# Four interleaved attention layers on one core: 288 score columns per unit in both sliding layers, cut as large bursts in 32x64 tiles and one small burst

## The chip, the cores and the metric

The kernel runs on one core of one Trainium2 chip. The metric is device time in microseconds (us) of one execution; lower is better. The core has a matrix engine (TensorE, PE in the profile, with its weight loads listed apart as PEld), a vector engine (DVE), a scalar engine (ACT), GpSimd (POOL) and a queue engine (SP) that issues DMAs. Each engine plays a list of instructions in a fixed order and waits on semaphores for the others.

## The reference

x is 2048 tokens by 512 features in bfloat16. Four residual layers follow one another: linear attention A, sliding-window attention B, A again with the same weights, B again. Each normalises x first. There are 32 heads of 16 features, and the window of B is 256 tokens.

```python
def _B_ref(x, wqkv, wo):
    B, S, D = x.shape
    H = 32; Dh = D // H; W = 256
    qkv = (lambda x, *d: x.transpose(*d))((x @ wqkv).reshape(B, S, 3, H, Dh), 2, 0, 3, 1, 4)
    q, k, v = qkv[0], qkv[1], qkv[2]
    scores = jnp.einsum("bhqd,bhkd->bhqk", q, k) * (Dh ** -0.5)
    idx = jnp.arange(S)
    mask = (idx[:, None] - idx[None, :] >= 0) & (idx[:, None] - idx[None, :] < W)
    scores = jnp.where(mask[None, None], scores, -1e9)
    p = _softmax(scores, axis=-1)
    o = jnp.einsum("bhqk,bhkd->bhqd", p, v)
    return (lambda x, *d: x.transpose(*d))(o, 0, 2, 1, 3).reshape(B, S, D) @ wo
...
x = A_x
x = x + _A_ref(_layernorm(x, axis=-1), A_wqkv, A_wo)
x = x + _B_ref(_layernorm(x, axis=-1), B_wqkv, B_wo)
x = x + _A_ref(_layernorm(x, axis=-1), A_wqkv, A_wo)
x = x + _B_ref(_layernorm(x, axis=-1), B_wqkv, B_wo)
```

A is the usual linear attention with the feature map elu + 1; the change does not touch it.

## The kernel before

The tokens lie in 16 tiles of 128. A unit of a sliding layer is one tile j of 128 keys: two blocks b of 64 keys, four feature groups f, and four heads of each group in four strips of 32 partitions (gq). For each unit the kernel computes scores of the unit's keys against the queries that can see them, turns them into exponentials, masks the edges, and multiplies with the values. Keys of one block are laid out so that a score column is one query and the 128 rows of a score tile are 64 keys of two heads (32 keys in rows 0 to 63, the other 32 in rows 64 to 127). Column c of block b belongs to the query 128 j + 64 b + c. A block of 64 keys and a window of 256 has scores in columns 0 to 319: columns 0 to 63 are cut by the causal edge ("near"), columns 256 to 319 by the far edge. Of these edges, the first 32 keys have nothing in columns 288 to 319, and the other 32 keys nothing in columns 0 to 31.

**First sliding layer** (phase 2 in the code, `merged` false). `b_scores` makes four large bursts a unit, one for each pair of feature groups `fs` and each block b: eight matmuls of 256 columns (0 to 255) in 32x128 tiles, that is, four strips side by side and each strip twice. Two exponentials on ACT (line 648) of 1024 elements a row follow, and one masking multiply on DVE (line 656). `b_far` makes one burst a unit for columns 256 to 319 of all groups and blocks: 32 matmuls of 64 columns in 32x128 tiles (line 677), two exponentials of 1024 elements (line 690), and two far masks `mf` on POOL or DVE (lines 708 and 709). So 320 columns are held for a block.

**Second sliding layer** (phase 3, `merged` true). The large bursts begin at column 32 and hold 224 columns (32 to 255), 896 elements an exponential. The far burst is cut in 32x64 tiles (line 680, 64 matmuls of 64 columns): the second half of the keys takes columns 256 to 319, the first half takes columns 256 to 287 and, in the place of its empty columns 288 to 319, its near columns 0 to 31. So 288 columns are held. A masking multiply for each (fs, b) (line 700) then moves these near columns to their place and applies the triangle to columns 0 to 63; the far masks `mf` follow it and clear what is left of them in columns 288 to 319.

The last two units of each sliding layer (j = 14 and 15, at the end of the tokens) have no far burst and take the plain form in both layers.

**Values.** `b_values` (line 729) multiplies the exponentials of up to three units (j, j-1, j-2) with the values, in two halves h of two feature groups, by matmuls of 34 columns. It waits for the exponentials and the masks of these units, and for far masks of unit j-2. Exponentials live in a ring `P` of `rp` slots, a slot a unit: three slots in the first sliding layer, four in the second. An exponential of unit j+3 in a ring of three may not be written before the values of unit j+2 have read the same slot.

**Order.** All instructions of all layers form one graph. A planner has laid out ahead of time in which order each engine plays its list, which engine does work that can be done on two, and in which of the eight PSUM banks each result lies; this comes to the kernel as a compressed table (`TABLE`, read by `place`). A score burst holds four of the banks until both its exponentials have read them. Between the steps of a sliding layer the planner puts work of the layers around it: projections of later tiles (lines 406 and 420), layer norms, and the next layer's key features. A burst stands between work in full 128x128 tiles, so PE changes its tile mode on the way in and on the way out.

Of the kernel before, what the change touches and what calls it, by code (L numbers as in the profile page):

```python
# [11 lines left out]
P = 128  # L12
D = 512
# [210 lines left out]
class Plan:  # L224
# [398 lines left out]
    def b_scores(self, j, b, fs, key):  # L623

        K = self
        ps = [Tile(1, "S") for _ in range(4)]
        skip = 32 if self.merged and j + 2 < T else 0
        q = P * j + 64 * b + skip
        ns = min(256 - skip, S - q)
# [3 lines left out]
        def put(e):  # L633
            m = None
            for i, f in enumerate(fs):
                for gq in range(4):
                    rows = slice(32 * gq, 32 * gq + 32)
                    m = e.matmul(K.ps(ps[gq])[:, ns * i:ns * i + ns], K.kB[rows, j % 4, 2 * f + b, :, :], K.XQ[rows, f, q:q + ns], start=True, stop=True, tile_position=(32 * gq, 0))  # L638
            return m

        self.pe("s", put, key, 1, ns * len(fs), mode=(32, 128), rd=[("kB", j % 4, 0), ("kB", j % 4, 1)] + [("XQ", t) for t in range(j, last + 1)], ps=ps)
# [9 lines left out]
        if skip:  # L651
            return
# [7 lines left out]
    def b_far(self, j, key):  # L660

        K = self
        merged = self.merged
# [3 lines left out]
        def put(e):  # L667
            m = None
            for f in range(4):
                for b in range(2):  # L670
                    q = P * j + 64 * b
                    c = 128 * f + 64 * b
                    for gq in range(4):
                        rows = slice(32 * gq, 32 * gq + 32)
                        x = K.XQ[rows, f, q + 256:q + 320]
                        if not merged:
                            m = e.matmul(K.ps(ps[gq])[:, c:c + 64], K.kB[rows, j % 4, 2 * f + b, :, :], x, start=True, stop=True, tile_position=(32 * gq, 0))  # L677
                            continue
                        for half in range(2):
                            m = e.matmul(K.ps(ps[gq])[64 * half:64 * half + 64, c:c + 64], K.kB[rows, j % 4, 2 * f + b, 32 * half:32 * half + 32, :],  # L680
                                         x if half else bass.AP(x.tensor, x.offset, [x.ap[0], [-256, 2], [1, 32]]), start=True, stop=True, tile_position=(32 * gq, 64 * half))
            return m

        self.pe("s", put, key, 1, 512, mode=(32, 64) if merged else (32, 128), occ=245, rd=[("kB", j % 4, 0), ("kB", j % 4, 1), ("XQ", j + 2)] + [("XQ", j)] * merged, ps=ps)
        sl = j % self.rp
        for h in range(2):
            def ex(e, h=h):
                i = span(ps[2 * h:2 * h + 2], lambda x: [[128, 4], x, [64, 2], [1, 64]])
                o = bass_view(K.P(sl)[:, 0, h, 256:320], [[1408, 8], [384, 2], [1, 64]])
                return e.activation(o.rearrange("p (f g) b c -> p f g b c", g=2), i, ACT.Exp, bias=0.0, scale=0.25)  # L690

            self.on("ACT", "ex", ex, key + 0.01 * h, act(1024), wr=[("F", sl, h)], rd=[("P", sl, 0)], ps=[ps[2 * h], ps[2 * h + 1]])

        for fs in ((0, 1), (2, 3)) if merged else ():
            for b in range(2):
# [6 lines left out]
                self.on("DVE", "mk", mk, key + 0.02 + 0.01 * b + 0.2 * fs[0], dve(512, "2x"), rd=[("P", sl, f, b, h) for f in fs for h in range(2)] + [("F", sl, 0), ("F", sl, 1), ("tri",)],  # L702
                        wr=[("P", sl, f, b, 2) for f in fs] + [("near", sl, b, fs[0])])
        for b in range(2):
# [7 lines left out]
            self.g.add("mf", engs, mk, key + 1.5 + 0.01 * b, rd=[("F", sl, 0), ("F", sl, 1), ("tri",)] + [("near", sl, b, 0), ("near", sl, b, 2)] * merged, wr=[("F", sl, b, 1)])  # L712

    def b_values(self, j, h, key):
# [6 lines left out]
        for f in (2 * h, 2 * h + 1):  # L721
# [13 lines left out]
            if j >= 2:  # L735
                rd += [("F", (j - 2) % K.rp, h_) for h_ in (0, 1)] + [("F", (j - 2) % K.rp, h_, 1) for h_ in (0, 1)]
# [51 lines left out]
    def middle(self, ph):  # L788
# [7 lines left out]
        self.merged = last  # L796
# [29 lines left out]
        for j in range(T):  # L826
# [7 lines left out]
            if j + 2 < T:  # L834
                self.b_far(j, base + j + 0.8)
# [24 lines left out]
    r"c-qZa1K1|VvaT*P*0yciwr$(CZQHhO+qTW@CcDXcb7%hV<eVfoo0F4!@AKUGhSk+o?^{*fGyMUCh3765goc+c9E6835CI|rLPAiG2oggihztY|-3#}`C",  # L860
# [210 lines left out]
```

## Time and profile before

| | us |
|---|---|
| median of 2 runs | 412.61 (411.49 to 413.72) |
| span of the profiled execution, first to last instruction | 408.2 |
| first linear layer and what leads to the first score burst | 0 to 62 |
| first sliding layer, score bursts to values | 62 to 222 |
| second linear layer | 222 to 257 |
| second sliding layer | 257 to 402 |

Of the profiled execution the page tells the span; the median of the runs is 4.4 us above it, which is launch and end around the span. A profile row names a line of the kernel, an engine, an operation, output <- inputs, the shape, and a count; then the busy time and the mean duration of one. Durations of matmuls overlap, since matmuls are pipelined: what a group of matmuls costs PE is the distance from its first start to the first start of the next group. The time of a stage is read from rows that cut the span into stretches.

### The profile page before, as it was taken

Reading aid. Unit: us, or ns where it says so; the run is one execution under the profiler, and the core shown is the slowest. Engines: PE = TensorE matmul, PEld = TensorE weight load, DVE = VectorE, ACT = ScalarE, POOL = GpSimd, SP = SyncE. Lnnn points to the kernel's source line nnn. Section 1 sums busy time; section 2 is a strip of 40 time slices with the busy share of each in tenths; the row PEclk is TensorE's granted clock in tenths of the full one; section 3 lists DMA queues with packets and bytes.
Section 4 is the critical chain, followed back from the end, with each engine's and each line's share of the span. In section 5 each row is a group of like instructions: output and inputs, shape, how many; then the busy total and the mean of one; then the engine's idle time right before and its main releaser. Section 6 shows DMA issues by size and latency. Waiting matters only on the chain.

```text
span 408.2 us, 18082 instructions
## 1 busy us (share of the span) xinstructions
PE 396.0 (97%) x7997; PEld 263.4 (65%) x7997; DVE 347.9 (85%) x808; ACT 344.4 (84%) x443; POOL 113.8 (28%) x194
## 2 busy tenths in 40 slices
PE   8999999999999999999999999999999999999996
PEld 3654676666575566666666777676757766576664
DVE  5998799999998999888977789988898778876685
ACT  3655579999999999999998355999998999999992
POOL 3553632112253343330503202122123201302212
PEclk9999999999999999999999999999999999999999
DMA  8754014923242934344231100364225542442543
GB/s 247 243 118 104 2 42 121 184 56 97 65 119 52 132 73 108 75 104 106 62 69 36 29 2 28 89 127 78 71 76 130 143 83 61 66 121 62 118 109 104
DMA packets 67654, 37.88 MB, mean 93 GB/s; under 512 B 48248, under 2 KB 62712, under 8 KB 67576
## 3 DMA queue, kind: packets, MB, share of 16 engines
q1 hardware_dynamic: 67184, 35.67, 38.1%
q8 instruction: 63, 1.03, 1.1%
q0 software_dynamic: 384, 1.05, 0.8%
q14 instruction: 15, 0.12, 0.1%
q10 hardware_dynamic: 8, 0.00, 0.0%
HBM read 6.29 MB, written 2.10 MB: 21 GB/s over the span
## 4 chain that ended last, share of the span: by engine, by line
PE 81%; ACT 10%; DVE 7%; DMA 1%; issue 1%; DVEq 0%
PE ps L406 27%; PE ps L420 20%; PE ps L729 15%; PE ps L638 8%; ACT pb L648 7%; PE ps L680 2%; PE ps L481 2%; ACT pb L690 1%; DVE XQ L563 1%; PE ps L677 1%; DMA XQ<-vp 1%; PE ps L984 1%; PE ps L457 1%; PE ps L543 1%; PE ps L268 1%
## 5 line engine op out<-in xcount | busy, mean ns | idle before, releaser
L648 ACT ACTIVATE pb<-ps 128x1024 bf16<-128x1024 f32 (+3 forms) x224 | 198.2, 966 | 7.4 <-PE ps L638 6.2
L729 PEld LDWEIGHTS ps<-vB,pb 128*128 128x128 bf16 x2560 | 77.6, 96 | 11.5 <-issue 4.2
L729 PE MATMUL ps<-vB,pb 128*128 128x34 bf16 x2560 | 83.2, 177 | 0.3
L420 PE MATMUL ps<-xT,wBp 128*128 128x128 bf16 x1024 | 68.6, 219 | 0.1
L420 PEld LDWEIGHTS ps<-xT,wBp 128*128 128x128 bf16 x1024 | 58.4, 98 | 9.6 <-issue 4.0
L708 POOL TENSOR_SCALAR_AFFINE_SELECT pb<-pb 128x1024 bf16<-128x1024 bf16 x34 | 39.1, 1149 | 84.0 <-DVE pb L700 31.9
L429 ACT ACTIVATE tE<-ps 128x512 bf16<-128x512 f32 x64 | 38.1, 606 | 18.4 <-PE ps L406 12.1
L638 PE MATMUL ps<-XQ,kB 32*128 32x256 bf16 (+2 forms) x1024 | 48.7, 262 | 3.3 <-ACT pb L648 0.6
L574 DVE TENSOR_TENSOR xres<-ps,xres 128x512 bf16<-128x512 f32 x63 | 43.1, 685 | 9.6 <-PE ps L406 9.1
L690 ACT ACTIVATE pb<-ps 128x1024 bf16<-128x1024 f32 x50 | 49.0, 1048 | 1.3 <-PE ps L680 1.0
L406 PE MATMUL ps<-wA,XQ 128*128 128x512 bf16 x192 | 49.2, 380 | 0.7 <-DMA XQ<-vp 0.6
L369 POOL TENSOR_SCALAR ve<-mv 128x1 f32<-128x1 f32 x49 | 11.8, 240 | 127.9 <-DVE mv L368 126.9
L370 POOL TENSOR_TENSOR rs<-ve,negh 128x1 f32<-128x1 f32 x64 | 37.9, 592 | 32.0 <-DVE ve L369 27.5
L367 DVE BATCH_NORM_STATS2 stats<-xres 128x6 f32<-128x512 bf16 x64 | 43.8, 685 | 2.8 <-DMA xres<-in_A_x_dram 2.1
L638 PEld LDWEIGHTS ps<-XQ,kB 32*128 32x128 bf16 x1024 | 15.7, 92 | 31.4 <-ACT pb L648 8.3
L420 PE MATMUL ps<-XQ,wA 128*128 128x128 bf16 x512 | 34.4, 219 | 0.0
L406 PE MATMUL ps<-wBv,xT 128*128 128x512 bf16 x128 | 34.3, 380 | 0.0
L406 PE MATMUL ps<-M,XQ 128*128 128x512 bf16 x128 | 33.3, 380 | 0.2
L420 PEld LDWEIGHTS ps<-XQ,wA 128*128 128x128 bf16 x512 | 30.1, 98 | 5.1 <-issue 0.6
L406 PE MATMUL ps<-wBo,oT 128*128 128x512 bf16 x124 | 32.7, 380 | 0.6 <-DVE vp L431 0.4
L656 DVE TENSOR_TENSOR pb<-pb,tri 128x512 bf16<-128x512 bf16 x68 | 27.7, 419 | 3.7 <-ACT pb L648 3.1
L741 DVE TENSOR_TENSOR o<-ps,rc 128x256 bf16<-128x256 f32 x64 | 27.0, 422 | 1.7
(114 smaller groups left out, 545.9 us busy)
## 6 DMA issues: line engine op xcount, KB each, us to landing
vB<-vS SPq DMA_DIRECT2D x64, 136.0 KB, 2.6
kB<-vp SPq DMA_DIRECT2D x64, 128.0 KB, 2.2
wA<-in_A_wqkv_dram SPq DMA_DIRECT2D x3, 512.0 KB, 5.2
xres<-in_A_x_dram SPq DMA_DIRECT2D x2, 512.0 KB, 4.8
pb<-in_B_wqkv_dram SPq DMA_DIRECT2D x1, 1024.0 KB, 6.9
out_dram<-xres POOLq DMA_DIRECT2D x8, 128.0 KB, 2.5
out_dram<-xres SPq DMA_DIRECT2D x7, 128.0 KB, 2.0
xres<-in_A_x_dram SPq DMA_DIRECT2D x3, 256.0 KB, 5.3
```

The source lines that it names most:

```text
L367: self.on("DVE", "stats", lambda e: e.bn_stats(K.stats[:, t, :], K.xres[:, t, :]), key, dve(512), rd=[("xres", t)], wr=[("stats", t)])
L370: self.pow = self.on("POOL", "pow", lambda e: e.tensor_tensor(K.rs[:, t, :], K.ve[:, t, :], K.negh[:], ALU.pow), key + 0.03, (640, 690), r ...
L406: m = e.matmul(K.ps(ps), lhs(c), rhs(c), start=c == 0, stop=c == 3)
L420: m = e.matmul(K.ps(ps)[:, f * P:(f + 1) * P], w(c, f), xT(c), start=c == 0, stop=c == 3)
L429: self.on("ACT", "E", lambda e: e.activation(K.tE[:, s, :], K.ps(ps), ACT.Exp, bias=0.0), key, act(512), wr=[("tE", s)], ps=[ps])
L574: self.on("DVE", "res", lambda e: e.tensor_tensor(K.xres[:, t, :], K.ps(po), K.xres[:, t, :], ALU.add), key, dve(512), rd=[("xres", t)], w ...
L638: m = e.matmul(K.ps(ps[gq])[:, ns * i:ns * i + ns], K.kB[rows, j % 4, 2 * f + b, :, :], K.XQ[rows, f, q:q + ns], start=True, stop=True, ti ...
L648: return e.activation(out(h, ns).rearrange("p (f g) c -> p f g c", f=n), i, ACT.Exp, bias=0.0, scale=0.25)
L656: return e.tensor_tensor(x, x, K.tri[:, 0, :].unsqueeze(1).to_broadcast([P, 4 * n, 64]), ALU.mult)
L690: return e.activation(o.rearrange("p (f g) b c -> p f g b c", g=2), i, ACT.Exp, bias=0.0, scale=0.25)
L708: return e.affine_select(out=x, in_=x, compare_op=ALU.is_ge, fill=0.0, base=-2, pattern=[[0, 16], [-2, 64]], channel_multiplier=1)
L729: m = e.matmul(K.ps(ps)[:, 34 * u:34 * u + 34], K.P((b // 2) % rp)[:, f, gq % 2 * 2 + gq // 2, o:o + P], K.vB[:, (b // 2) % 4, b % 2, r, : ...
```

## The change

Both sliding layers now hold 288 columns, and they do it in another cut. `b_scores` makes large bursts that begin at column 64 (`skip = 64`) and hold 256 columns in 32x64 tiles: the second half of the keys takes columns 64 to 319, the first half columns 64 to 287, and eight more matmuls of 32 columns put the first half's near columns 0 to 31 in the place of its columns 288 to 319. The far burst goes; in its place `b_near` makes one small burst for columns 32 to 63 of both halves, in 32x128 tiles: 32 matmuls of 32 columns, two exponentials of 512 elements. The masking multiplies and far masks are those of the merged form in both layers; the values of a unit wait for the small burst of that unit (`N`) where they waited for the far burst two units back (`F`). `self.merged` goes. The planner's table is a new one: the orders, the choice of engines and the banks are all new.

```diff
     def b_scores(self, j, b, fs, key):
...
-        skip = 32 if self.merged and j + 2 < T else 0
+        merged = j + 2 < T
+        skip = 64 if merged else 0
         q = P * j + 64 * b + skip
-        ns = min(256 - skip, S - q)
+        ns = min(256, S - q)
...
             for i, f in enumerate(fs):
                 for gq in range(4):
                     rows = slice(32 * gq, 32 * gq + 32)
-                    m = e.matmul(K.ps(ps[gq])[:, ns * i:ns * i + ns], K.kB[rows, j % 4, 2 * f + b, :, :], K.XQ[rows, f, q:q + ns], start=True, stop=True, tile_position=(32 * gq, 0))
+                    if not merged:
+                        m = e.matmul(K.ps(ps[gq])[:, ns * i:ns * i + ns], K.kB[rows, j % 4, 2 * f + b, :, :], K.XQ[rows, f, q:q + ns], start=True, stop=True, tile_position=(32 * gq, 0))
+                        continue
+                    for half in (1, 0):
+                        n = 224 + 32 * half
+                        m = e.matmul(K.ps(ps[gq])[64 * half:64 * half + 64, 256 * i:256 * i + n], K.kB[rows, j % 4, 2 * f + b, 32 * half:32 * half + 32, :], K.XQ[rows, f, q:q + n],
+                                     start=True, stop=True, tile_position=(32 * gq, 64 * half))
+            for i, f in enumerate(fs) if merged else ():
+                for gq in range(4):
+                    rows = slice(32 * gq, 32 * gq + 32)
+                    m = e.matmul(K.ps(ps[gq])[0:64, 256 * i + 224:256 * i + 256], K.kB[rows, j % 4, 2 * f + b, 0:32, :], K.XQ[rows, f, q - 64:q - 32], start=True, stop=True, tile_position=(32 * gq, 0))
             return m
...
-        self.pe("s", put, key, 1, ns * len(fs), mode=(32, 128), rd=..., ps=ps)
+        self.pe("s", put, key, 1, ns * len(fs), mode=(32, 64) if merged else (32, 128), rd=..., ps=ps)
...
-    def b_far(self, j, key):
+    def b_near(self, j, key):
...
                 for b in range(2):
                     q = P * j + 64 * b
-                    c = 128 * f + 64 * b
+                    c = 64 * f + 32 * b
                     for gq in range(4):
                         rows = slice(32 * gq, 32 * gq + 32)
-                        x = K.XQ[rows, f, q + 256:q + 320]
-                        if not merged:
-                            m = e.matmul(K.ps(ps[gq])[:, c:c + 64], K.kB[rows, j % 4, 2 * f + b, :, :], x, start=True, stop=True, tile_position=(32 * gq, 0))
-                            continue
-                        for half in range(2):
-                            m = e.matmul(K.ps(ps[gq])[64 * half:64 * half + 64, c:c + 64], ..., tile_position=(32 * gq, 64 * half))
+                        m = e.matmul(K.ps(ps[gq])[:, c:c + 32], K.kB[rows, j % 4, 2 * f + b, :, :], K.XQ[rows, f, q + 32:q + 64], start=True, stop=True, tile_position=(32 * gq, 0))
...
-            self.on("ACT", "ex", ex, key + 0.01 * h, act(1024), wr=[("F", sl, h)], rd=[("P", sl, 0)], ps=[ps[2 * h], ps[2 * h + 1]])
+            self.on("ACT", "ex", ex, key + 0.01 * h, act(512), wr=[("N", sl, h)], rd=[("P", sl, 0)], ps=[ps[2 * h], ps[2 * h + 1]])
...
-                self.on("DVE", "mk", mk, ..., rd=[("P", sl, f, b, h) for f in fs for h in range(2)] + [("F", sl, 0), ("F", sl, 1), ("tri",)],
+                self.on("DVE", "mk", mk, ..., rd=[("P", sl, f, b, h) for f in fs for h in range(2)] + [("N", sl, 0), ("N", sl, 1), ("tri",)],
...
-            self.g.add("mf", engs, mk, key + 1.5 + 0.01 * b, rd=[("F", sl, 0), ("F", sl, 1), ("tri",)] + [("near", sl, b, 0), ("near", sl, b, 2)] * merged, wr=[("F", sl, b, 1)])
+            self.g.add("mf", engs, mk, key + 1.5 + 0.01 * b, rd=[("P", sl, f, b, h) for f in range(4) for h in range(2)] + [("near", sl, b, 0), ("near", sl, b, 2), ("tri",)], wr=[("F", sl, b, 1)])
...
             if j >= 2:
-                rd += [("F", (j - 2) % K.rp, h_) for h_ in (0, 1)] + [("F", (j - 2) % K.rp, h_, 1) for h_ in (0, 1)]
+                rd += [("F", (j - 2) % K.rp, h_, 1) for h_ in (0, 1)]
+            rd += [("N", j % K.rp, h_) for h_ in (0, 1)] * (j + 2 < T)
...
             if j + 2 < T:
-                self.b_far(j, base + j + 0.8)
+                self.b_near(j, base + j + 0.8)
...
 TABLE = (
...
```

126 lines of the change are left out of this document (60 added, 66 removed).

## The prediction

> **What bounds the kernel now.** I read the page first: busy times, the granted clock and the chain that ended last.
>
> ```profile
> span 408.2 us, 18082 instructions
> PE 396.0 (97%) x7997; PEld 263.4 (65%) x7997; DVE 347.9 (85%) x808; ACT 344.4 (84%) x443; POOL 113.8 (28%) x194
> ...
> PEclk9999999999999999999999999999999999999999
> ...
> PE 81%; ACT 10%; DVE 7%; DMA 1%; issue 1%; DVEq 0%
> ```
>
> PE is idle for 408.2 - 396.0 = 12.2 us in all, its clock is full throughout, and four fifths of the chain are its own. Next I cut the span at the two sliding stages, the only places that the change touches.
>
> ```profile
> core 0: us, PE busy (x) PEld busy (x) DVE busy (x) ACT busy (x) POOL busy (x), PEclk, DMA share, GB/s
> 62.00:222.00 160.00, 157.93 (x3203) 101.65 (x3202) 143.20 (x334) 155.25 (x184) 48.23 (x72) 1.00 0.43 92
> 257.00:402.00 145.00, 140.31 (x3597) 97.99 (x3596) 118.74 (x272) 136.16 (x169) 29.86 (x42) 1.00 0.42 95
> ```
>
> In the first sliding stage PE (157.9 of 160) and ACT (155.3) are both full; in the second PE has 4.7 us of idle time, ACT 8.8. A busy matrix engine need not be a fast one, so I looked in the timeline at what it does in between. The rows are of the first stage, then of the second; first column start, second length with the tail of the last matmul.
>
> ```profile
> 172.75 0.41 PE L677 MATMUL ps<-XQ,kB 32*128 32x64 bf16 x32
> 173.09 1.04 PE L406 MATMUL ps<-wBo,oT 128*128 128x512 bf16 x4
> 173.96 1.06 PE L420 MATMUL ps<-xT,wBp 128*128 128x128 bf16 x16
> 174.95 0.40 PE L638 MATMUL ps<-XQ,kB 32*128 32x256 bf16 x8
> 175.28 1.37 PE L729 MATMUL ps<-vB,pb 128*128 128x34 bf16 x48
> 176.58 0.40 PE L638 MATMUL ps<-XQ,kB 32*128 32x256 bf16 x8
> ```
>
> ```profile
> 300.75 0.37 PE L638 MATMUL ps<-XQ,kB 32*128 32x224 bf16 x8
> 301.05 0.60 PE L406 MATMUL ps<-wBv,xT 128*128 128x512 bf16 x2
> ...
> 302.18 0.71 PE L680 MATMUL ps<-XQ,kB 32*64 32x64 bf16 x64
> 302.82 0.22 PE L729 MATMUL ps<-vB,vp 128*128 128x34 bf16 x2
> ```
>
> From start to next start, four matmuls of 512 columns take 0.87 us, that is 2.36 columns a ns; 48 value matmuls take 1.30, 27 ns each although 34 columns would stream in 14. Nothing stands still between them. So PE works at its pace, and each us of matrix time added in these stages is a us of the span, less whatever idle time it fills. The same rows price a burst as PE feels it: large with 256 columns 175.28 - 174.95 = 0.33 us, large with 224 columns 0.30, far burst 0.34 in the first stage and 0.64 in the second.
>
> **The change part by part.** Fourteen units a layer change. *Large bursts*, four a unit in both layers, go from 8 matmuls to 24, in tiles of half the width. No row shows this form, so I build it from the inside of two bursts. Cut into stretches that begin together at a burst's start, the trace counts (x) the matmuls begun so far:
>
> ```profile
> 152.24:152.25 0.01, 0.01 (x4) 0.01 (x6) 1.00 0.89 188
> 152.24:152.35 0.12, 0.12 (x4) 0.11 (x8) 1.00 1.00 203
> 152.24:152.37 0.13, 0.13 (x8) 0.11 (x8) 1.00 0.99 200
> ```
>
> ```profile
> 302.18:302.20 0.03, 0.02 (x8) 0.03 (x8) 1.00 0.00 0
> 302.18:302.29 0.11, 0.11 (x24) 0.11 (x31) 1.00 0.00 0
> 302.18:302.32 0.14, 0.14 (x31) 0.14 (x33) 1.00 0.00 0
> 302.18:302.42 0.24, 0.23 (x32) 0.23 (x33) 1.00 0.00 0
> 302.18:302.68 0.50, 0.49 (x63) 0.48 (x64) 1.00 0.00 0
> ```
>
> The first block is a large burst of 256 columns: four tiles at once, then nothing until 0.12, when the second round starts; that round streams 256 / 2.36 = 108 ns to about 0.24, and the next work starts at 0.33, so leaving the tile mode costs 0.09. The second block is the far burst in 32x64 tiles: 24 matmuls of 64 columns (27 ns each) have begun by 0.11, three rounds of eight tiles, though one strip of rows serves two of these tiles. So the two column halves stream side by side. Its last matmul starts at 0.50, streams 0.03, and the next work starts at 0.64: leaving this mode costs 0.11.
>
> Now the new burst. Eight matmuls start within 25 ns; the second eight follow when the 256 columns are through, 108 + 25 = 133 ns, the last of them at 157. Its first half has 224 columns, 95 ns, so that the last strip's small matmul of 32 columns starts at 252. The second small one of the same strip follows after some 30 ns (the far burst of the first layer has 8 rounds: 0.34 less 0.09 to leave and 0.03 for the last to stream, in 7 steps of about 31; value matmuls go at 27): 282, plus 14 to stream, 0.30; plus leaving. With the 32x128 exit of 0.09 that is 0.39, with the 32x64 exit 0.41; I take 0.41, since the mode is that one, and keep 0.385 to 0.42 as bounds. [...]
>
> *Far burst to small burst.* 32 matmuls of 32 columns in 32x128 tiles, where 64 columns take 0.34. If only the streams counted, seven steps would each be 13 ns shorter, 0.25; if nothing got shorter, 0.34. Value matmuls of 34 columns go at 27 ns and not at 14, so I take 0.31, nearer to the upper end.
>
> The sum for PE, a unit: first layer 4 x (0.41 - 0.33) + 0.31 - 0.34 = +0.29, second layer 4 x (0.41 - 0.30) + 0.31 - 0.64 = +0.11. Times 14: +4.1 and +1.5, together **+5.6 us**. By the bounds: 0.385 and 0.25 give +0.13 and -0.05 a unit, +1.1 in all; 0.42 and 0.34 give +0.37 and +0.18, +7.7.
>
> *ACT.* The rows, by shape:
>
> ```profile
> L648 ACT ACTIVATE pb<-ps 128x1024 bf16<-128x1024 f32 x120 | 114.6, 1036 | 3.5 <-PE ps L638 2.5
> L648 ACT ACTIVATE pb<-ps 128x896 bf16<-128x896 f32 x88 | 74.6, 927 | 3.4 <-PE ps L638 3.2
> L690 ACT ACTIVATE pb<-ps 128x1024 bf16<-128x1024 f32 x50 | 49.0, 1048 | 1.3 <-PE ps L680 1.0
> L648 ACT ACTIVATE pb<-ps 128x512 bf16<-128x512 f32 x4 | 2.3, 597 | 0.0
> L656 DVE TENSOR_TENSOR pb<-pb,tri 128x512 bf16<-128x512 bf16 x68 | 27.7, 419 | 3.7 <-ACT pb L648 3.1
> L700 DVE TENSOR_TENSOR pb<-pb,tri 128x512 bf16<-128x512 bf16 x44 | 17.4, 414 | 1.4 <-ACT pb L690 0.8 <-ACT pb L648 0.2
> ```
>
> In the first layer two exponentials a unit shrink from 1048 to some 597 ns: 28 x 0.45 = 12.6 us off ACT. In the second layer 8 x 896 + 2 x 1024 elements become 8 x 1024 + 2 x 512, the same 9216 in the same ten instructions: nothing. What the 12.6 us are worth is what PE waits in that stage, 160 - 157.9 = 2.1 us at most; half of it I credit, 1.0, since some of these waits are on DVE. In the second layer I credit none of the 4.7, and charge none.
>
> *At nothing.* Masks: 419 ns becomes 414 with the same count, on a DVE with 17 us free in the first stage (143.2 of 160). Far masks: they now wait for all exponentials of their unit, but are read two units later, and POOL is busy 48 of 160. Large bursts now read the queries of tile j+2 a little sooner than the far burst did; these are projected about a unit ahead by the code's keys; uncovered, it would cost a PE wait a unit. No DMA is added. The new wait of the values on the small burst has PE's whole list queued behind it, and behind the values stand the exponentials three units on in the first layer; hidden if the small burst is placed first in its unit, a rival below if not. The new orders cannot be read from the diff; their bound is PE's idle time, 2.1 + 4.7 us to win.
>
> Forecast: 412.6 + 5.6 - 1.0 = **417 us**. The profiled execution would go from a span of 408.2 to 412.8; I carry the same step over to the median, which lies 4.4 above the span. Own range of this case: +1.1 - 2.1 up to +7.7, 411.6 to 420.3, with some way beyond for what the order loses.
>
> **The rivals.** *The column halves of one strip take turns* (slower). Then a strip streams 2 x (256 + 224 + 32) = 1024 columns, 434 ns, with about 25 of start-up and 0.11 to leave 0.57: +0.93 and +0.75 a unit, +23.5 us, 436. Against it stand 24 starts in 0.11 us; for it, that the same burst is slow later on. It decides if the second round of eight starts at 0.21 and not at 0.13.
>
> *The values wait in the first layer* (slower). If the small burst stands at the end of its unit (its key in the code is j + 0.8), the values need its exponentials, two masks of 0.41 and 1.30 us of matmuls before exponentials of unit j+3 may write the slot: 2.1 us a unit without exponentials, 14 x 2.1 = 29. ACT then needs 155.3 - 12.6 + 29 = 172 against 160 + 4.1 of PE: 8 more than forecast, 425. For it: a ring of three and two full engines. Against it: the second layer's merged form has this wait already and loses 4.7 us with four slots. It decides when the small exponentials follow the last large ones of the unit.
>
> *The slow pace of the far burst's second part holds for the small matmuls.* Between 0.24 and 0.50 that burst starts 31 matmuls, 8.4 ns each, 67 a round instead of some 30. With 67, the two small rounds cost 2 x 37 = 74 ns more a burst: 112 x 0.074 = 8.3, 425. Against it: the slow pace sets in only after 32 matmuls, and the new burst has 24. [...]
>
> *PE idle time is recovered* (faster). With the low sum of +1.1 and an order that wins all 6.8 us of idle time, 407; if the planner also set bursts of one tile mode side by side and saved exits of 0.11 us for some forty of them, 402. For it: ACT is loosened in the stage where both engines are full. Against it: a burst holds four of eight banks, and it would take ACT as a reader without delay.
>
> **How the numbers follow.** About 2% (8.3 us: 404.4 to 420.9) is what a measurement of this kernel can tell from no change. Chances: forecast 0.47, of which 0.06 beyond 420.9 by a worse order; halves take turns 0.08; values wait 0.19; slow pace 0.07; idle recovered 0.19, of which 0.09 below 404.4. Faster 0.09, within 0.41 + 0.10 = 0.51, slower 0.06 + 0.08 + 0.19 + 0.07 = 0.40. The range from 405 to 430 leaves out the fastest case and the halves that take turns, 0.17, and a little of the long end of the waits.
>
> **What would show it.** The large burst in the new timeline: 0.41 us from its start to the next, the second eight begun at 0.13, the small ones from 0.25 on; the small burst 0.31; PE busy up by some 5 us; ACT in the first sliding stage down by 12 us and idle instead. A large burst over 0.45, an ACT as full as before, or PE idle for more than 12 us in all would make the prediction wrong in the size; a PE with fewer exits or with less matrix time than now, in the sign.

## The result, and the profile after

The changed kernel takes 431.32 us in the median (430.69 to 431.96) where the kernel before takes 412.61: 1.046 times as long, 95% interval 1.038 to 1.054. 417 was forecast, with 405 to 430 around it; the time lies outside.

The profiled execution has a span of 430.2 us, 22.0 more than before. Launch and end add 1.8 us to a span here (431.96 us for that execution), and 1.7 to 2.0 in every run below. So the 4.4 us between before's span and its median, given ahead as launch and end, are not that alone: the profiled execution of before was a shorter one than the two runs of its median. In the experiments below before takes 409.7 to 410.5 us, which fits its span.

The page of after: span, busy times, the instruction queue q8, the chain that ended last.

```profile
span 430.2 us, 20688 instructions
...
PE 390.9 (91%) x9260; PEld 284.3 (66%) x9341; DVE 346.1 (80%) x798; ACT 336.3 (78%) x445; POOL 119.6 (28%) x205
...
q8 instruction: 74, 1.21, 1.2%
...
PE 65%; ACT 13%; DVE 9%; DMA 8%; issue 4%; SPq 1%; POOL 0%; DVEq 0%; POOLq 0%
```

PE's share of the chain falls from 81% to 65%; transfers (1% to 8%), "issue" (time in which PE waits for nothing that the profile shows, 1% to 4%) and ACT (10% to 13%) take it over. 81 matmul records are missing (9260 against 9341 weight loads), which makes PE look idler than it is by some of its 39 us; the run below in which two places of SP's list are exchanged has every record, and PE busy 401.1 of 426.5, so 25 us idle where before has 12.

First the burst, by which the forecast stood or fell. Timeline of after, matmuls of the first sliding stage: a large burst, its eight small matmuls, the values behind it; and below, the small burst.

```profile
125.32 0.37 PE L686 MATMUL ps<-XQ,kB 32*128 32x32 bf16 x32
125.62 1.07 PE L420 MATMUL ps<-xT,wBp 128*128 128x128 bf16 x16
...
195.72 0.42 PE L645 MATMUL ps<-XQ,kB 32*64 32x256 bf16 x16
195.94 0.23 PE L650 MATMUL ps<-XQ,kB 32*64 32x32 bf16 x8
196.10 1.37 PE L734 MATMUL ps<-vB,pb 128*128 128x34 bf16 x48
```

From 195.72 to 196.10 are 0.38 us (median of the bursts 0.378), the small matmuls begin at 0.22; the small burst takes 0.30. Put into the forecast's own sum, this gives 14 x (4 x (0.378 - 0.33) + 0.303 - 0.34) = +2.2 us in the first layer and 14 x (4 x (0.378 - 0.30) + 0.303 - 0.64) = -0.4 in the second: matrix time grew by about 1.8 us, not by 5.6. Most of the loss is somewhere else.

So I followed PE operation by operation (an operation is a group of matmuls that stands at one place of PE's list): from the start of one to the start of the next, less the usual pitch of its kind and 96 ns at a change of tile mode. The usual pitches add up to PE's own work. What is over was put to whatever released the next operation last, or to "nothing" where all that it needs had come.

| PE's time, first to last operation, us | before | after | more |
|---|---|---|---|
| own work | 385.0 | 386.8 | 1.8 |
| waits for transfers (xT, XQ, kB, vB, oT) | 0.8 | 11.3 | 10.5 |
| waits for ACT | 4.3 | 8.8 | 4.5 |
| waits for DVE | 4.8 | 6.4 | 1.6 |
| released by nothing | 3.3 | 7.0 | 3.7 |
| small remainders | 1.2 | 1.5 | 0.3 |
| together (rounded) | 399.3 | 421.7 | 22.4 |

By place: the first score burst starts at 67.7 us where before has 62.3, 5.4 later. Nothing of the cut is changed ahead of it. Four matmuls of 512 columns and 32 of 128 more stand there now, some 2.6 us of work that is only moved; the rest is waiting. From the first burst to the last values the first sliding stage takes 7.5 us more (171.5 for 164.0), the second 6.7 more (152.1 for 145.4), although its own work became cheaper.

The view of waits says the same in its rows. PE's weight loads that waited for transfers, before and then after (us in total, times, longest):

```profile
PEld ps L406 <- DMA XQ<-vp: 1.1, 1, 1.1
...
PEld ps L420 <- DMA wA<-in_A_wqkv_dram: 0.3, 1, 0.3
```

```profile
PEld ps L406 <- DMA oT<-o: 3.9, 3, 1.8
...
PEld ps L420 <- DMA XQ<-vp: 2.0, 1, 2.0
...
PEld ps L734 <- DMA vB<-vS: 1.6, 1, 1.6
...
PEld ps L406 <- DMA XQ<-xn: 1.3, 2, 1.2
...
PEld ps L406 <- DMA XQ<-vp: 0.5, 1, 0.5
...
PEld ps L645 <- DMA kB<-vp: 0.2, 1, 0.2
```

And ACT's exponentials, waiting for the burst, before and after:

```profile
ACT pb L648 <- PE ps L638: 6.2, 15, 0.7
```

```profile
ACT pb L660 <- PE ps L650: 20.1, 36, 1.9
```

ACT is less busy (344.4 to 336.3 us; the exponentials alone take 12 us less, as forecast, and ACT took over other work), and waits three times as long for bursts. Part of it is that a burst ends later for its readers: where an exponential waited for nothing else, it starts 0.45 us (256 columns) or 0.42 (224) after the first matmul of a burst of 8 (before), 0.56 after that of a burst of 24 (after), though PE itself is free 0.05 to 0.08 later only.

Last, one thing in the timeline of after that no wait can explain:

```profile
338.96 0.32 PE L686 MATMUL ps<-XQ,kB 32*128 32x32 bf16 x23
340.53 0.23 PE L686 MATMUL ps<-XQ,kB 32*128 32x32 bf16 x9 [1.25 <-issue]
```

This is one operation of 32 matmuls. It waits for other engines ahead of its first matmul, nowhere else; yet PE stops after 23 and goes on 1.25 us later. I come back to it.

### The profile page after: what moved, and what is told of

Its sections match the earlier page's. It is cut to its first block, busy times and chain, and to the rows that moved or that the text cites. A ratio compares the mean times of both kernels' runs of the same rounds, so it can differ in the third digit from the quotient of the medians.

```text
span 430.2 us, 20688 instructions
## 1 busy us (share of the span) xinstructions
PE 390.9 (91%) x9260; PEld 284.3 (66%) x9341; DVE 346.1 (80%) x798; ACT 336.3 (78%) x445; POOL 119.6 (28%) x205
## 4 chain that ended last, share of the span: by engine, by line
PE 65%; ACT 13%; DVE 9%; DMA 8%; issue 4%; SPq 1%; POOL 0%; DVEq 0%; POOLq 0%
PE ps L406 20%; PE ps L420 16%; PE ps L734 13%; ACT pb L660 11%; PE ps L645 7%; DMA XQ<-vp 2%; DMA XQ<-xn 2%; DMA oT<-o 2%; DVE stats L367 2%; PE ps L686 1%; PE ps L481 1%; PE ps L650 1%; DMA vB<-vS 1%; DMA xres<-in_A_x_dram 1%; ACT pb L695 1%
## 5 line engine op out<-in xcount | busy, mean ns | idle before, releaser
L660 ACT ACTIVATE pb<-ps 128x1024 bf16<-128x1024 f32 (+2 forms) x224 | 208.0, 1005 | 24.1 <-PE ps L650 20.1
L713 POOL TENSOR_SCALAR_AFFINE_SELECT pb<-pb 128x1024 bf16<-128x1024 bf16 x38 | 44.3, 1166 | 77.9 <-DVE pb L705 60.5
L645 PE MATMUL ps<-XQ,kB 32*64 32x256 bf16 (+1 forms) x1792 | 47.7, 273 | 4.6 <-ACT pb L660 1.6
L406 PE MATMUL ps<-wA,XQ 128*128 128x512 bf16 x176 | 45.9, 379 | 4.1 <-DMA XQ<-vp 1.6
L705 DVE TENSOR_TENSOR pb<-pb,tri 128x512 bf16<-128x512 bf16 x100 | 40.8, 427 | 7.2 <-ACT pb L695 3.6
L645 PEld LDWEIGHTS ps<-XQ,kB 32*64 32x64 bf16 x1792 | 18.1, 102 | 29.7 <-ACT pb L660 8.7
L406 PE MATMUL ps<-wBo,oT 128*128 128x512 bf16 x100 | 28.0, 380 | 8.0 <-ACT pb L660 2.1
L746 DVE RECIPROCAL rc<-ps 128x16 f32<-128x16 f32 x64 | 16.2, 253 | 22.2 <-PE ps L734 21.6
L695 ACT ACTIVATE pb<-ps 128x512 bf16<-128x512 f32 x50 | 27.6, 616 | 5.5 <-PE ps L686 5.2
L406 PE MATMUL ps<-M,XQ 128*128 128x512 bf16 x113 | 29.0, 379 | 2.8 <-issue 1.4
```

Of the source, the lines that this page charges most:

```text
L406: m = e.matmul(K.ps(ps), lhs(c), rhs(c), start=c == 0, stop=c == 3)
L645: m = e.matmul(K.ps(ps[gq])[64 * half:64 * half + 64, 256 * i:256 * i + n], K.kB[rows, j % 4, 2 * f + b, 32 * half:32 * half + 32, :], K.X ...
L660: return e.activation(out(h, ns).rearrange("p (f g) c -> p f g c", f=n), i, ACT.Exp, bias=0.0, scale=0.25)
L705: return e.tensor_tensor(o, x, t, ALU.mult)
L713: return e.affine_select(out=x, in_=x, compare_op=ALU.is_ge, fill=0.0, base=-2, pattern=[[0, 16], [-2, 64]], channel_multiplier=1)
```

## The experiments

Two theories at first. *The orders*: the five lists in the new table are worse. *The cut*: bursts of 24 and the waits that come with them. Each run is given as a ratio to the kernel before, timed on the same chip (409.7 to 410.5 us there).

### One part at a time

**Before's cut in after's lists.** Before's operations in the relative order, on the engines and in the banks that after's table gives (where the cuts differ, the old far burst takes the small burst's place; 19 of PE's operations had to move, by 8 places at most).

```diff
 TABLE = (
-... before's orders, engines, banks
+... after's, for before's operations
```

> The scores are cut as in the kernel before (320 columns in the first sliding layer, 288 in the second); orders, engines and banks are those of the changed kernel's table, with the far burst in the place of the small one. The burst cut costs PE only 1.6 us more by the two traces. If the new orders lose the time (the theory): 427 to 431 us, about what the changed kernel takes. If the new cut loses it: 411 to 416. If the wait of the values on the small burst loses it, in the first sliding layer alone: about 424.

449.82 us, ratio 1.097 (1.090 to 1.103). Slower than either kernel. PE's waits for ACT are 28.9 us where before has 4.3.

**The new cut in the second sliding layer alone, before's lists.**

```diff
+NEW = (3,)
+    def b_scores(self, *a):
+        return (self.b_scores_new if self.new else self.b_scores_old)(*a)
```

> The kernel before in its own order, with the new cut in the second sliding layer only, where the instructions match one to one. Orders theory: 412 us, 0.5 us less than before (14 units x (4 x 0.075 - 0.335)). Cut theory: the second sliding layer is 6.7 us longer in the changed kernel, so 419.

423.86 us, ratio 1.034 (1.029 to 1.038). That stage goes from 145 to 158 us. Own work falls by 0.8 us, waits for ACT rise from 4.3 to 17.2.

**The new cut in both layers, before's lists,** the small burst third of its unit.

```diff
+NEW = (2, 3)
```

> The new cut in both sliding layers, laid into the order of the kernel before: the small burst stands third in its unit, in the first sliding layer the bursts behind it move by one slot, and masks and values follow as late as they must. Orders theory: 414 us for the cut, and up to 4 more for what is moved without a planner. Cut theory: 428 to 433. Values-wait theory: about 421.

582.2 us, ratio 1.419 (1.413 to 1.425). In the first sliding stage, now 317 us, PE waits at each unit for values, masks and the transposed output in turn. The granted matrix clock plays a part too, here in tenths over 40 equal slices of the span:

```profile
PEclk9999996787775667985797779599989999999999
```

**Before, with the first linear layer in after's order.** Only this layer's operations change their places, engines and banks.

> The kernel before; only the operations of the first linear layer take the order, engines and banks among themselves that they have in the changed kernel. No score burst is changed. Orders theory: the first score burst comes 5.4 us later, as in the changed kernel, 418 us. Cut theory: 412.6.

438.6 us, ratio 1.069 (1.064 to 1.074). The first score burst starts at 67.5 us, as in after (67.7; before 62.3), and the first sliding stage, whose lists are untouched, loses 23 more.

Both theories missed, and by far. Counted at the usual pitches PE's own work is 384.2 to 385.4 us in all four runs, so an order acts through waits. That count hides one more thing, the granted clock, which is full throughout before and after. With the new cut in both layers it stands at half for 161 of 580 us; a matmul of 512 columns then takes 0.43 us instead of 0.22, and such slow matmuls of full tiles alone make some 27 us of that run's loss. Before's cut in after's lists and the exchanged first linear layer have it at half for about 14 us each, the run with the new cut in the second layer alone for 3.4. Lists that fit one cut don't fit another, nor another start of the same kernel (28.9 and 17.2 us of waits for ACT where before has 4.3, and 23 us lost in a stage whose lists are untouched): every engine plays its list in order, and an operation that is late in one list holds up all that stands behind it. Transplants measure this misfit and neither theory. What can be compared are runs that leave the lists alone.

### The burst alone, lists untouched

**After with bursts of 16.**

```diff
-                        n = 224 + 32 * half
+                        n = 256
...
-            for i, f in enumerate(fs) if merged else ():
+            for i, f in ():
```

> After with its lists untouched; every large burst is issued as 16 matmuls of 256 columns in 32x64 tiles, without the eight of 32 columns (so keys 0 to 31 get columns 288 to 319 where the diagonal's first 32 belong; the exps, masks and values are as many and as large as before). Burst theory (the 24 matmuls hold PE 0.378 us where 16 hold 0.33, and free the exps about 0.1 us later, and the lists are so tight that all of it shows): a replay of the lists with the durations of the traces loses 5.3 us, so 424 to 427 where after has 431. Theory of the lists and their landings (the burst costs little, the new lists meet late transfers): the lists stay, so 429 to 433, unless the shift happens to move a late landing off the path.

426.7 us, ratio 1.041 (1.038 to 1.044); after has 1.046 (1.038 to 1.054), so the intervals overlap. In the two profiles the span falls by 4.8 us, of which own work is 2.4.

**Before with bursts of 24,** on the columns that before has.

```diff
+                    for half in (1, 0):
+                        w = ns - 32 + 32 * half
+                        m = e.matmul(K.ps(ps[gq])[64 * half:64 * half + 64, ns * i:ns * i + w], ..., tile_position=(32 * gq, 64 * half))
+            for i, f in enumerate(fs) if halves else ():
+                for gq in range(4):
+                    rows = slice(32 * gq, 32 * gq + 32)
+                    m = e.matmul(K.ps(ps[gq])[0:64, ns * i + ns - 32:ns * i + ns], ..., tile_position=(32 * gq, 0))
```

> Before with its own lists, cut, exps and masks; each large burst of both sliding layers is issued in the changed kernel's form, 16 matmuls in 32x64 tiles and eight of 32 columns, on the columns that before has. Burst theory: the replay goes from 404.7 to 412.9 us, so +8, 418 to 421 where before has about 410 to 412; if the whole loss of the change were the burst, +18.7, 429. Theory of the lists: the matrix time grows by about 6 us (112 bursts by 0.05 to 0.07 us) and a part of it goes into PE's idle time, so 412 to 417, and the rest of the change's loss is not in the burst.

423.5 us, ratio 1.032 (1.030 to 1.035): 13.0 us from the burst's form, with the order, the cut, ACT's and DVE's work as before. PE's own work grows by 5.4. Its waits for transfers (0.8 to 1.3) and ACT (4.3 to 5.1) hardly grow; "released by nothing" goes from 3.3 to 8.3. The page and the timeline of this run:

```profile
PE 403.1 (96%) x9789; PEld 288.0 (68%) x9789; DVE 348.4 (83%) x808; ACT 346.8 (82%) x443; POOL 114.2 (27%) x194
...
q8 instruction: 77, 1.26, 1.3%
...
PE 81%; ACT 9%; DVE 4%; DMA 3%; issue 2%; SPq 0%; DVEq 0%
```

```profile
353.49 0.25 PE L740 MATMUL ps<-vB,pb 128*128 128x34 bf16 x4
353.78 0.39 PE L644 MATMUL ps<-XQ,kB 32*64 32x224 bf16 x13
354.92 0.28 PE L644 MATMUL ps<-XQ,kB 32*64 32x192 bf16 x3 [0.75 <-issue]
354.93 0.31 PE L649 MATMUL ps<-XQ,kB 32*64 32x32 bf16 x8
```

Again a burst broken in the middle. The packets of queue q8 are 16,384 bytes each, and their number goes with PE's instructions: 63, 74 and 77 packets for 7,997, 9,341 and 9,789 pairs of weight load and matmul in before, in after and here. That is a packet for 126 to 127 pairs, or about 64 bytes an instruction, an estimate from these counts. Nine times in this run PE stands for 0.25 to 1.1 us with nothing to release it, all in the second sliding stage; each time the next matmul starts 1.3 to 1.9 us after the end of a packet on q8, 51 to 102 pairs after the packet began. My reading, which no run shows by itself, is that PE had run through the instructions it held: a packet takes about 1 us (median 1.05 in before and in after), and 1.3 to 1.9 more pass until PE goes on, while 70 pairs of values at 25 ns are gone in 1.75 us and a burst's 24 pairs in 0.38, an estimate from the pitches.

The other profiles show the same interval. In before, after and the eight runs of this section and the next one, from the first score burst on, PE has 49 such standstills of over 0.25 us (leaving out places ahead of a 512-column matmul, where lost records leave gaps too: all 81 that after lacks are of such matmuls). 47 of them end 1.25 to 2.0 us after the end of a packet on q8, though a packet comes only every 6.2 us in before and every 5.6 in after, on average. A run with 60 to 63 packets has 0 to 2 of them, one with 65 or 67 has 3 or 4, one with 70 to 77 has 6 to 9.

**Before with longer values,** PE time without many instructions.

```diff
-                        m = e.matmul(..., start=i == 0, stop=i == len(blocks) - 1)
+                        for again in (True, False) if i == 0 and gq < 2 else (False,):
+                            m = e.matmul(..., start=i == 0, stop=again or i == len(blocks) - 1)
```

> Before with its own lists; in each of the 256 values operations of the two sliding layers the first matmul of two heads is issued twice (the second overwrites the first), 2 x 256 matmuls in all at most by 25 ns, so at most 12.8 us of PE time if all 256 operations count and 6.4 us if 128 do: about the matrix time that the burst of 24 added in the run before (112 bursts by 0.047 us are 5.3 us, and the time grew by 13.0), with a seventh of its instructions. Theory that PE waits for its instructions (in the run with bursts of 24, PE stood still eight times for 0.3 to 1.1 us, 6.1 us in all, in the second sliding layer, with nothing that releases it, and each time went on 1.6 to 2.1 us after the end of an instruction transfer): time grows by the PE time alone, 1.0 us for each us added, and no such stalls, about 417 for 6.4 us. Theory that any matrix time costs double in lists this tight: 2 us for each us added, about 423.

419.98 us, ratio 1.024 (1.023 to 1.026). There are 128 such operations, so 256 matmuls (8253 against 7997 in the profile) and 6.4 us of own work, for which the time grew by 9.9: between the two theories. The rest is waits for transfers (0.8 to 3.0), DVE (4.8 to 6.0) and 1.2 us more released by nothing. A us of matrix time cost 1.5 us here, and the burst of 24, with less matrix time, costs 3 us more.

**Before with bursts of 16.**

```diff
-                        w = ns - 32 + 32 * half
+                        w = ns
...
+            for i, f in ():
```

> Before with its own lists, cut, exps and masks; each large burst is issued as 16 matmuls in 32x64 tiles, without the eight small ones (all columns are there). Matrix time: 0.357 us against 0.330 in the first sliding layer, as much more in the second, 112 by 0.027 or 3.0 us; 896 matmuls more, half of the burst of 24. Theory that PE waits for its instructions: half of the standstill too, 2 to 3 us, so 415 to 417 where before has 410.5. If the eight small matmuls alone make the loss (they end the burst 0.07 us later): 412 to 414.

420.43 us, ratio 1.025 (1.022 to 1.027). Own work +3.0 as expected, the time +10.3: more than the 4.5 to 6.5 expected. Released by nothing: 7.6 us, nearly what the burst of 24 has, with half of its extra matmuls. The standstills therefore don't grow in proportion to the instructions; why not was not shown.

**After with bursts of 8.**

```diff
-                    if not merged:
+                    if True:
...
-            for i, f in enumerate(fs) if merged else ():
+            for i, f in ():
...
-        self.pe(..., mode=(32, 64) if merged else (32, 128), ...)
+        self.pe(..., mode=(32, 128), ...)
```

> After with its lists untouched; every large burst is issued as before's first layer does it, eight matmuls of 256 columns in 32x128 tiles (so keys 0 to 31 get columns 288 to 319 where the diagonal's first 32 belong; exps, masks and values as many and as large). It takes 1,792 matmuls out of 9,341 and 112 by 0.048 us of matrix time. If the burst's form is the larger part (its matrix time, its later end, and PE's waits for instructions): 10 to 13 us less, 418 to 421. If after's lists are the larger part: the 5 us of the replay, 425 to 427.

419.25 us, ratio 1.023 (1.021 to 1.025): half of the loss goes, as the burst theory has it. The other half stays (9.1 us), though PE's own work (381.1 us) is 3.9 below before's and its matmuls fewer:

```profile
PE 398.7 (94%) x7549; PEld 259.1 (61%) x7549; DVE 345.7 (82%) x798; ACT 335.9 (80%) x445; POOL 118.9 (28%) x205
...
q8 instruction: 60, 0.98, 0.9%
...
PE 61%; ACT 19%; DVE 10%; DMA 7%; issue 1%; SPq 1%; POOL 0%; ACTq 0%; DVEq 0%
```

```profile
PEld ps L420 <- DMA XQ<-vp: 2.5, 1, 2.5
...
PEld ps L406 <- DMA oT<-o: 2.2, 3, 1.1
...
PEld ps L734 <- DMA vB<-vS: 1.0, 1, 1.0
...
PEld ps L641 <- DMA kB<-vp: 0.7, 1, 0.7
```

"Issue" is back at 1% of the chain. What is left are the same kinds of waits as in after, for transfers (8.4 us, before 0.8) and for ACT (9.8, before 4.3). They belong to after's lists or to the rest of its cut, the small burst and the masks behind it, which this run keeps. (The profiled execution took 424.29 us; its clock is at half for 6.8 us, which cost some 3 if half of that was lost, my estimate.)

### The lists alone, same operations

Each of these two was picked by replaying the five lists with the durations of the traces and landings drawn at random.

**After, lists shifted locally.**

> After with the same operations, engines and PSUM banks; PE's, ACT's, DVE's and SP's lists shifted locally (232 of PE's 868 places differ, by 13 places at most), picked for the least mean of a replay with landings drawn at random (414.0 us where after's lists have 415.8). Theory of the lists and their landings: after's lists lose some 12 us more on the chip than the replay has, because transfers land late just where they are waited for; lists that stand elsewhere lose less, 414 to 422. Burst or cut theory: what the cut costs is in any lists of this kind, so 428 to 433.

427.17 us, ratio 1.041 (1.035 to 1.047). That is not the 414 to 422 expected, and the intervals do not tell it from after's 1.046. In its profile waits for transfers fall from 11.3 to 4.3 us; own work, ACT and standstills are as in after. In its view of waits:

```profile
PEld ps L406 <- DMA XQ<-vp: 1.2, 2, 1.0
...
PEld ps L406 <- DMA XQ<-xn: 1.0, 1, 1.0
...
PEld ps L406 <- DMA oT<-o: 0.4, 1, 0.4
```

**Before, lists shifted locally.**

> Before with the same operations, engines and banks; the lists shifted locally in the same manner (177 of PE's 868 places, by 17 at most; replay mean 405.5 us where before's own lists have 408.0). If the replay decides: 1 to 3 us below before, 408 to 411. If before's lists are fitted to the landings that they really meet: 2 to 8 us above before, 413 to 420.

415.37 us, ratio 1.012 (1.007 to 1.017), where the replay promised a gain of 2.5 us: waits for DVE 8.4 (before 4.8) and for transfers 4.0. A small shift of lists cost about 5 us here, and the replay didn't see it coming.

**After, the first transpose ahead of a weight load on SP's list.**

```diff
 SP: ... x6, x8,
-wBn, T, x12, T, ...
+T, wBn, x12, T, ...
```

> After; on SP's list alone the first transpose by DMA goes ahead of the 1 MB weight load that stands before it (it took 6.0 us to land behind that load, 2.4 to 2.8 where nothing is ahead). Theory of the lists and their landings: PE's standstill of 1.5 us at 17 us goes, so 1 to 3 us less, 428 to 430. If that wait is made up later: 431, no change.

429.52 us, ratio 1.047 (1.045 to 1.050): no change that the intervals can tell from after's 1.046. PE's waits for transfers in the first linear layer are 3.9 us, in after 3.5. The wait wasn't removed but moved: two later transposes, issued behind the load, now land after 6.2 and 6.7 us, where after's took 3.7 and 4.5. So this run doesn't show what that landing is worth.

### Instructions alone

**Before with idle waits on PE,** eight and then sixteen ahead of each of 449 linear operations.

```diff
+                    if name == "PE" and o.name in ("bq", "bk", "bv", "bout", "k", "v", "g", "aout"):
+                        for _ in range(8):
+                            e.wait_ge(wsem, 1)
```

> Before with its own lists, bursts and data; ahead of each of 449 linear operations on PE stand eight waits on a semaphore that was reached at the start. They compute nothing and wait for nothing: 3,592 instructions more for PE, as many as the burst of 24 added (3,584), without its matrix time. Theory that PE's instruction transfers are a cost of their own (they leave PE standing, and data transfers land late where they share the engines: 50% of those that meet one in flight against 5% of the others, over seven runs): 14 transfers of 16 KB more (77 for 63), PE standing 3 to 6 us, late landings more in number, 414 to 419 where before has about 410.3. If the standing came from the bursts themselves, from their matrix time and their later end: at most what the waits take to issue (17 ns each on other engines, most of it beside running matmuls), 410 to 412.

> The same with 16 waits ahead of each of the 449 operations: 7,184 instructions more, 28 transfers (91 for 63). Theory of the instruction transfers: twice the loss of the run with eight or a little over, 418 to 428. If the loss is the waits' own issue: in proportion too, but without standing after instruction transfers and without more late landings; if neither, 410 to 413.

429.29 us, ratio 1.048 (1.044 to 1.051), and 592.32 us, ratio 1.443 (1.439 to 1.448). Both far beyond any theory, and for another reason: half as many instructions were made of them as expected, 1,796 and 3,592 (the profiles count 19,878 and 21,674 instructions where before has 18,082; q8 has 70 and 77 packets), and each takes 51 ns, which is also the median of the 200 semaphore instructions of PE's list in before's trace. PE's rows in the two views of waits, eight and sixteen:

```profile
PE ps L406 <- issue: 2.3, 8, 0.6
PE ps L420 <- issue: 1.9, 6, 0.4
PE ps L729 <- issue: 1.5, 2, 1.2
```

```profile
PE ps L406 <- issue: 62.8, 195, 0.8
PE ps L420 <- issue: 26.6, 80, 0.6
```

Eight are 4 x 51 = 204 ns and sixteen 408; PE shows the second in full (about 0.4 us at each of 449 places; the span grew by 182.6 us) and a part of the first. These runs don't separate instruction supply from the waits' own time, as they were meant to. The run with eight holds one hint: standstills of 0.4 to 1.3 us that end 1.3 to 1.8 us after a packet's end, with bursts as in before, which itself has one of 0.6.

## Why the prediction was wrong

**The matrix term was mis-sized, to the high side.** "The sum for PE ... together +5.6 us" measured +1.8. A large burst takes 0.378 us, not 0.41: the last small matmul starts at 0.267 and not at 0.282, and from there the next work is 0.11 away and not 0.128. Less the 14 ns of streaming, leaving the mode took 0.096, so the step from 0.09 to 0.11 that the forecast read off the far burst is hardly there. The small burst (0.30) was right. The halves of a strip stream side by side (the second eight matmuls begin 0.123 us after the first, not 0.21), so the 436 us rival was rightly put low; the slow pace (0.067 a round) did not bite within the burst either (the two rounds of small matmuls begin 0.03 apart).

**The step that failed is another,** since the smaller matrix term would have moved the forecast further from the result: "The new orders cannot be read from the diff; their bound is PE's idle time, 2.1 + 4.7 us to win." PE's idle time bounds what an order can win. It says nothing of what an order can lose, and the forecast kept 0.06 for that. The same operations in other lists gave +4.9 us (before, shifted), +28.9 (before's first layer exchanged) and +40 (after's lists), the last two with some of the time at half clock. In after, 16.6 of 22.4 us are PE's waits for transfers, ACT and DVE; with the burst of 8 put back, 9.1 us of the loss remain. That PE already waits more in the first linear layer, where the cut plays no part, points to the lists; that all of the 9.1 us are theirs, and none the small burst's, is argued and not shown.

**The second omission: a burst was priced by PE's time alone.** In before's lists the burst of 24 has 5.4 us of matrix time and costs 13.0. About 5 of the difference are standstills without a releaser. The rest fits the price of 1.5 us for each us that the values' run showed. (With bursts of 16 the same sum, 4.5 and 4.3 us, gives 8.8 of the 10.3 measured.) The forecast's "each us of matrix time added in these stages is a us of the span" was too low by that factor in the one run that measured it. My reading, which no run isolates, is that an operation that ends later is also met later by ACT (0.56 us after a burst's start where it was 0.42 to 0.45), by DVE and by the transfers behind them.

The two halves agree with each other: 13.0 us from the burst in before's lists, about 9 left with the burst of 8, together 22. The spans differ by 22.0; the medians by 18.7, with an interval of 15.7 to 22.2 from two runs each.

**Points that held.** ACT did become less busy; yet PE's waits for ACT rose by 4.5 us, where the forecast credited 1.0. "PE idle for more than 12 us in all would make the prediction wrong in the size": 25 where every record is there. The rival of the values that wait for the small burst did not happen in after: PE waited 0.3 us in all for that mask, its weight loads 3.1. Its 425 us came near by chance.

**What stays open.** That instruction packets leave PE standing is not shown; the reading rests on bursts broken in mid-operation, on the steady 1.25 to 2.0 us after a packet's end, and on the number of standstills, which follows the number of packets over ten profiles (0 to 2 with 60 to 63 packets, 6 to 9 with 70 to 77); the instructions added to take no time took 51 ns each, and reducing them at equal matrix time wasn't tried. Which places in after's lists cost the 9 us is known by what PE waits for and not by an edit that takes them away, and whether the small burst has a part in them wasn't tried; a list as good for this cut as before's is for its own may exist, and wasn't found.

## What to carry to other kernels

In a kernel whose engines play hand-fitted lists, price a change of order from both sides: idle time bounds the gain, while every short wait that a list leaves uncovered is a loss, and one layer in another order cost 29 us here. Ask of an operation not only how long it holds its engine but when its readers may start (0.56 against 0.42 to 0.45 us) and how many instructions it needs (the burst of 24 cost 3 us more than the longer values, with less matrix time). To tell a part from its order, edit the operation and leave the lists alone; transplanting a list to other operations measures the misfit.

## What the runs showed of the hardware

**PE stands still at times, and goes on at a steady time after an instruction packet.** The packets of 16 KB on q8 are 63 in before, 74 in after, 77 with bursts of 24 in before. Standstills of over 0.25 us without a releaser add up to 0.6, 6.0 and 6.3 us in these three, and 47 of the 49 in ten profiles end 1.25 to 2.0 us after the end of such a packet. That PE waits for what the packet brings was not shown.

**Transfers that met an instruction packet landed late more often.** I call a transpose, a key copy or a value copy late when it takes over 1 us more than the shortest time of its kind (2.4, 1.9 and 2.4 us). The packets of 8 KB on q14, the other instruction queue, count too. Over all sixteen profiles, 825 of the 1,915 transfers that met an instruction packet within that shortest time after their issue were late, and 48 of the 1,387 that met none there; in before alone 53 of 118 and 1 of 93, in after 62 of 137 and 5 of 75. (The same stretch for all: otherwise a late transfer meets more packets because it is late.) An example of after, where PE then waits for the transposed output:

```profile
144.83 1.24 SPq L377 DMA_TRANSPOSE oT<-o  x1
...
149.27 0.11 PEld L406 LDWEIGHTS ps<-wBo,oT 128*128 128x128 bf16 x2 [1.81 <-DMA oT<-o]
```

Between the two, instruction packets were under way from 145.85 to 146.45 and from 147.21 to 148.31 us, and packets of 256 bytes, the transposes' (43,008 for 84 of them), 18 ns in the median, took up to 1.13 us. The count is a correlation; no run changed the packets alone.

**A wait that is already met is not free on PE:** 51 ns each here. Eight in a row, 3,592 in all, lengthened the span by 182.6 us, which is 51 ns for each; four in a row, 1,796 in all, lengthened it by 19.0 us.

**The granted clock halved inside one execution.** It was full throughout before and after. Its mean was 0.861 over the 579.9 us of the run with the new cut in both layers (at half for 161 us; there the pitch of 512-column matmuls went from 0.216 to 0.427 us), and 0.996 and 0.992 over the runs with the new cut in the second layer alone and with bursts of 8 in after (at half for 3.4 and 6.8 us). No run here isolates what sets it off.
